# Retention attention in whole units, with smaller decay tables, and matmul operands at multiples of 512 bytes

## The chip, the cores and the metric

One NeuronCore of one Trainium2 chip. Times are microseconds (us) of device time for one execution. A measurement is the median of several runs.

## The reference, cut to what matters

Inputs: q, k and v with 4 batches, 8 heads, 576 positions and 64 dims, and the weights of two expert stages. All is float32.

```python
scores = matmul(q, k^T) / sqrt(64)
Dmat   = where(rel >= 0, gamma[h] ** rel, 0)      # rel = row - column, gamma[h] = 1 - 2**(-5-h)
x      = matmul(scores * Dmat, v)                 # no softmax; heads side by side: [2304, 512]
x      = relu(x @ w_in)**2 @ w_out                # first MoE: 512 -> 2048 -> 512
p      = probs / (sum(probs) + 1e-9)
out    = sum over 4 experts e of p[:, e] * (relu(x @ w1[e]) @ w2[e])     # 512 -> 1024 -> 512
```

## The kernel before

**Attention** (lines 136 to 334) takes two heads of a batch as a unit: 16 units, n = 0 to 15. Positions are cut in five chunks c of 128, the last of 64 (`CH`). As the decay is a power of gamma, the part of a chunk that looks at earlier chunks goes through a running state of 64x64 per head: `update` (L231) adds k^T v of a chunk to a state in PSUM with start and stop flags over four chunks, and two ScalarE copies (L248) take a snapshot of it, one for each head, before the next update adds to the same place. `outer` (L269) multiplies the snapshot with the scaled queries. The part inside a chunk is `scores` (L203), the decay mask by VectorE (`masked`, L218), and `inner` (L253), masked scores times v. `finish` (L281) rounds the sum to float32r on ScalarE (`xh`) and keeps the rest by a VectorE subtraction (`xl`). Heads j = 0 and 1 lie in the two halves of the partitions or of the columns.

A unit is done in two steps, h = 0 with chunks 0 to 2 and h = 1 with chunks 3 and 4. The loop from L309 issues for each step an update, the next step's scores and masks, the values of all chunks of the step but the last, a second update, the last chunk's values, the outer products, and `finish`. The fifth chunk's values use 64 of the 128 rows (L266). Scores have K = 64 rows, all other matmuls of attention 128.

`load` (L160) fetches a unit three ahead, from SyncE's queue (from ScalarE's for unit 0), into tiles with three buffers. In the first four units it also fetches that head pair's tables: a mask of 192 columns, whose last 64 repeat the first, and the query decay for 448 positions. `prepare` (L186) scales k and q on GpSimd. The expert weights arrive as float64 words: from unit 3 on `tick` advances a generator (L68, L101) that rebuilds them on VectorE, ScalarE and GpSimd, three steps per unit.

**MoE** (L356 on). Every operand is split into a high and a low float32r part, and each product is three matmuls. Weights go in 24 chunks c of two 128-wide slices of the inner dimension: 8 of the first MoE, 16 of the second. Tokens go in five groups g, four of 512 and one of 256. `layer1` (L365) has the weights w1 stationary and x moving, 24 matmuls a group. `layer2_1` (L389) has w2 stationary and the activations g moving, 24 matmuls. `layer2_2` (L418) has g stationary and w2 moving with 512 columns, six matmuls for each 128 tokens. Layer 2 of one group follows layer 1 of the next.

**Where tiles lie.** Pools are laid out one behind the other in each partition: 16 KB that are kept back, four constants of 32 bytes, then `xh` and `xl` (L42), the pieces of weights (`wrp`, `cvp`, `wp`), and then the tiles of attention, and in the same place, once it is over, those of MoE (L341 to L347): the accumulators, `pr` (288 bytes), `prsum` (96), and `ghi`, `glo`, `r`. In the built program xh starts at byte 16512, which is 32 x 512 + 128; the first buffer of whi at 123008, which is 240 x 512 + 128; the first of ghi at 193024, which is 377 x 512.

Of the kernel before, what the change touches and what calls it, by code (L numbers as in the profile page):

```python
# [6 lines left out]
F32 = mybir.dt.float32  # L7
# [3 lines left out]
ACTF = mybir.ActivationFunctionType  # L11
ALU = mybir.AluOpType
PSUM = bass.MemoryType.PSUM
# [19 lines left out]
def tile_kernel(ctx, tc, qT, kT, kn, vn, v4d, mask, qdec, kdec, wd, w, probs, out):  # L33
    nc = tc.nc
    const = ctx.enter_context(tc.tile_pool(name="const", bufs=1))
    xp = ctx.enter_context(tc.tile_pool(name="xp", bufs=1))
    wrp = ctx.enter_context(tc.tile_pool(name="wrp", bufs=4))
    cvp = ctx.enter_context(tc.tile_pool(name="cvp", bufs=1))
# [8 lines left out]
    def f32(ap):  # L47
        return ap.bitcast(F32)
# [87 lines left out]
    def attention(a):  # L136
# [3 lines left out]

        ap = a.enter_context(tc.tile_pool(name="ap", bufs=3))
        ac = a.enter_context(tc.tile_pool(name="ac", bufs=1))
        pq = a.enter_context(tc.tile_pool(name="pq", bufs=2, space=PSUM))
        px = a.enter_context(tc.tile_pool(name="px", bufs=2, space=PSUM))
        pst = a.enter_context(tc.tile_pool(name="pst", bufs=2, space=PSUM))

        mk = ac.tile([C, NP, 2, MW], F32, name="mk")
        qd = ac.tile([128, NP, S - C], F32, name="qd")
        kd = ac.tile([C, NP, 4, 2], F32, name="kd")
        v4 = ac.tile([64, B * NP, 2, D], F32, name="v4")  # L150

        kts = [ac.tile([128, NC_ * C], F32, name=f"kt{i}") for i in range(3)]

        sbs = [ac.tile([128, 2, D], F32, name=f"st{i}") for i in range(6)]

        units = [(b, a) for b in range(B) for a in range(NP)]
        NU = len(units)
# [2 lines left out]
        def load(n):  # L160
            if n >= NU:
                return
            b, a = units[n]
            q_t = ap.tile([128, S], F32, name="q_t")
            k_t = kts[n % 3]
            k_n = ap.tile([C, 4, 2, D], F32, name="k_n")
            v_n = ap.tile([C, 4, 2, D], F32, name="v_n")

            dma = nc.scalar if n == 0 else nc.sync
            nc.sync.dma_start(out=q_t, in_=qT[b, a])  # L170
            dma.dma_start(out=k_t[:, :S], in_=kT[b, a])
            if n == 0:
                dma.dma_start(out=kd, in_=kdec)
            if n < NP:
                nc.sync.dma_start(out=mk[:, a], in_=mask[:, a])
            dma.dma_start(out=k_n, in_=kn[b, a].rearrange("p (c h d) -> p c h d", c=4, h=2))
            nc.sync.dma_start(out=v_n, in_=vn[b, a].rearrange("p (c h d) -> p c h d", c=4, h=2))
            if a == 0:
                dma.dma_start(out=v4[:, b * NP : (b + 1) * NP], in_=v4d[b].rearrange("p (a h d) -> p a h d", a=NP, h=2))
            if n < NP:  # L180
                nc.sync.dma_start(out=qd[:, a], in_=qdec[:, a])
            tl[n] = (q_t, k_t, k_n, v_n)

        qs = {}

        def prepare(n):  # L186

# [7 lines left out]
            qs[n] = ap.tile([128, S - C], F32, name="q_s")  # L195
            nc.gpsimd.tensor_tensor(out=qs[n], in0=q_t[:, C:], in1=qd[:, a, :], op=ALU.mult)

        steps = [(n, h) for n in range(NU) for h in range(2)]
        CS = [(0, 1, 2), (3, 4)]
        qks, pts, sts, snaps = {}, {}, {}, {}  # L200
        snap_n = [0]

        def scores(s):  # L203
            n, h = s
            q_t, k_t, _, _ = tl[n]
            qk = pq.tile([C, 2, 512], F32, name="qk")
            for c in CS[h]:
                o, m = CH[c]
                w = o - CH[CS[h][0]][0]
                for j in range(2):  # L210
                    p = slice(64 * j, 64 * j + 64)
                    nc.tensor.matmul(  # L212
                        qk[:, j, w : w + m], k_t[p, o : o + C], q_t[p, o : o + m], start=True, stop=True,
                        skip_group_check=True,
                    )
            qks[s] = qk

        def masked(s):  # L218
            n, h = s
            a = units[n][1]  # L220
            qk = qks.pop(s)
            pt = ap.tile([C, 2, 3 * C], F32, name="pt")
            if h == 0:
                v = lambda t: t[:, :, : 3 * C].rearrange("p j (c i) -> p j c i", c=3)
                m = mk[:, a, :, :C].unsqueeze(2).to_broadcast([C, 2, 3, C])
                nc.vector.tensor_tensor(out=v(pt), in0=v(qk), in1=m, op=ALU.mult)
            else:
                nc.vector.tensor_tensor(out=pt[:, :, :MW], in0=qk[:, :, :MW], in1=mk[:, a], op=ALU.mult)  # L228
            pts[s] = pt

        def update(n, c):  # L231

            if n >= NU:
                return
            _, _, k_n, v_n = tl[n]
            if c == 0:
                sts[n] = pst.tile([128, D], F32, name="state")
            st = sts[n]
            for j in range(2):
                nc.tensor.matmul(  # L240
                    st[64 * j : 64 * j + 64, :], k_n[:, c, j, :], v_n[:, c, j, :],
                    start=(c == 0), stop=(c == 3), skip_group_check=True,
                )
            sb = sbs[snap_n[0] % len(sbs)]
            snap_n[0] += 1
            for j in range(2):
                p = slice(64 * j, 64 * j + 64)
                nc.scalar.copy(out=sb[p, j, :], in_=st[p, :])  # L248
            snaps[n, c + 1] = sb

        xos = {}

        def inner(s, c):  # L253

            n, h = s
            v_n = tl[n][3]
            o, m = CH[c]
            w = o - CH[CS[h][0]][0]
            if c == CS[h][0]:
                xos[s] = px.tile([128, 512], F32, name="xo")  # L260
            xo, pt = xos[s], pts[s]
            for j in range(2):
                vc = v_n[:, c, j, :] if c < 4 else v4[:, n, j, :]
                nc.tensor.matmul(  # L264
                    xo[64 * j : 64 * j + 64, w : w + m], vc, pt[:m, j, w : w + m],
                    start=(w == 0), stop=(c == 0), skip_group_check=True,  # L266
                )

        def outer(s, c):  # L269

            n, h = s
            o, m = CH[c]
            w = o - CH[CS[h][0]][0]
            xo, sb = xos[s], snaps.pop((n, c))
            for j in range(2):
                nc.tensor.matmul(  # L276
                    xo[64 * j : 64 * j + 64, w : w + m], sb[:, j, :], qs[n][:, o - C : o - C + m],
                    start=False, stop=True, skip_group_check=True,
                )

        def finish(s):  # L281
            n, h = s
            b, a = units[n]
            o = CH[CS[h][0]][0]
            m = sum(CH[c][1] for c in CS[h])
            xo = xos.pop(s)
            t = b * S + o
            hi = xh_[:, a, t : t + m]
            nc.scalar.copy(out=hi, in_=xo[:, :m])  # L289
            nc.vector.tensor_tensor(out=xl_[:, a, t : t + m], in0=xo[:, :m], in1=f32(hi), op=ALU.subtract)  # L290
            pts.pop(s)

        load(0)
        warm = ac.tile([1, 1], F32, name="warm")
# [1 line left out]
        nc.scalar.copy(out=warm, in_=warm)  # L296
        for t in kts:
            nc.vector.memset(t[:, S:], 0.0)
        for t in sbs:
            nc.gpsimd.memset(t, 0.0)  # L300
        load(1)
        load(2)
        prepare(0)
        scores(steps[0])
        masked(steps[0])
        update(0, 0)
        prepare(1)
        update(0, 1)
        for i, s in enumerate(steps):  # L309
            n, h = s  # L310
            nxt = steps[i + 1] if i + 1 < len(steps) else None
            un, uc = (n, 2) if h == 0 else (n + 1, 0)
            update(un, uc)
            if nxt:
                scores(nxt)
                masked(nxt)
            cs = CS[h]
            for c in cs[:-1]:
                inner(s, c)
            update(un, uc + 1)  # L320
            inner(s, cs[-1])
            for c in cs:
                if c:
                    outer(s, c)
            finish(s)
            if h == 0:
                prepare(n + 2)
            else:
                load(n + 3)
            if h == 0 and n % 2 == 0 and 2 <= n < 2 + 2 * PC:  # L330
                load_piece(0, n // 2 - 1)
            if s == (3, 0):
                work.append(split_w(0))
            tick(1 + h)

    with tc.manual_schedule():
        with ExitStack() as a:
# [7 lines left out]
        yacc = [yp.tile([128, KT, GS[g]], F32, name=f"y{g}", tag=f"acc{g}") for g in range(NG)]  # L345
        pr = yp.tile([128, NTT, 4], F32, name="pr")
        psum_ = yp.tile([128, NTT], F32, name="prsum")  # L347
        nc.sync.dma_start(out=pr, in_=probs)
        nc.vector.tensor_reduce(out=psum_, in_=pr, axis=mybir.AxisListType.X, op=ALU.add)
        nc.vector.tensor_scalar_add(psum_, psum_, 1e-9)  # L350
# [95 lines left out]
def _host(inputs):  # L446
# [28 lines left out]
    gamma = (1.0 - 2.0 ** (-5.0 - np.arange(H))).reshape(NP, 2)  # L475
    rel = np.arange(C)[None, :] - np.arange(C)[:, None]
    mask = np.where(rel[:, None, None, :] >= 0, gamma[None, :, :, None] ** np.abs(rel)[:, None, None, :], 0.0) / 8.0
    mask = np.concatenate([mask, mask[..., : MW - C]], axis=3)
    qdec = np.repeat(gamma, D, axis=1).T[:, :, None] ** (np.arange(C, S) - S // 2)[None, None, :] / 8.0
    pos = np.arange(4)[None, :] * C + np.arange(C)[:, None]  # L480
    kdec = gamma[None, :, None, :] ** (S // 2 - pos)[:, None, :, None]
    f = np.float32
# [25 lines left out]
```

## Time and profile before

| | |
|---|---|
| median of 3 runs | 1288.08 us (1287.55 to 1289.81) |
| profiled execution | 1288.76 us, span 1286.5 us |
| granted TensorE clock, mean | 0.999 |
| TensorE busy | 1272.8 us, 99% |
| VectorE, ScalarE, GpSimd busy | 658.7, 299.0, 332.9 us |
| chain of waits by engine | PE 97%, DVE 1%, DMA 1% |

In the profile PE is TensorE, PEld its weight loads, DVE VectorE, ACT ScalarE, POOL GpSimd, and SP SyncE's DMA queue. L365 is line 365 of the kernel. "h<-xh,whi" reads as the tile written, then the tiles read. A float32 matmul of attention appears as two passes per matmul, so an instruction group "x4" at L240 is one update for two heads. Matmuls overlap, and the duration of a single one is longer than the time from its start to the next one's.

### The profile page before, as it was taken

The numbers are of one execution on the slowest core, as the hardware profiler recorded it, in microseconds if no ns is written. First come the engines' busy times: TensorE is split into PE (matmuls) and PEld (weight loads), VectorE is DVE, ScalarE is ACT, GpSimd is POOL, SyncE is SP. The second block draws the span as 40 slices with busy tenths as digits, with TensorE's granted clock in tenths as the row PEclk, the third lists the DMA queues.
The fourth block names the chain that finished last, engine by engine and source line by source line (L and its number), as shares of the span: only waits on it lengthen the run. The fifth ranks groups of instructions, "written<-read, shape, count | busy, mean of one in ns | idle before, by whom it ended". The sixth has DMA issues, their size and how long they took to land.

```text
span 1286.5 us, 16159 instructions
## 1 busy us (share of the span) xinstructions
PE 1272.8 (99%) x6720; PEld 1059.2 (82%) x6720; DVE 658.7 (51%) x946; ACT 299.0 (23%) x636; POOL 332.9 (26%) x270
## 2 busy tenths in 40 slices
PE   7999999999999999999999999999999999999998
PEld 6878888888888888888888888888888888888887
DVE  4965777887877851143343433434434433434334
ACT  3544322223222253311111111111111111111110
POOL 4654454444444592011010010110110110110100
PEclk9999999999999999999999999999999999999999
DMA  9931110111110000000000000000000000000003
GB/s 330 327 105 34 38 61 23 44 50 33 49 47 28 25 33 25 9 33 24 10 33 11 22 33 9 25 29 12 25 25 9 34 25 9 33 17 17 1 34 114
DMA packets 27465, 59.42 MB, mean 46 GB/s; under 512 B 3328, under 2 KB 4352, under 8 KB 27392
## 3 DMA queue, kind: packets, MB, share of 16 engines
q1 hardware_dynamic: 26880, 57.69, 13.1%
q8 instruction: 52, 0.85, 0.3%
q10 hardware_dynamic: 512, 0.70, 0.2%
q14 instruction: 21, 0.17, 0.0%
HBM read 53.66 MB, written 4.72 MB: 45 GB/s over the span
## 4 chain that ended last, share of the span: by engine, by line
PE 97%; DVE 1%; DMA 1%; ACT 0%; issue 0%; ACTq 0%; DVEq 0%
PE h L365 46%; PE o L418 31%; PE o L389 16%; PE xo L264 1%; PE qk L212 1%; PE xo L276 1%; PE state L240 1%; DMA v_n<-vn 1%; DMA k_n<-kn 0%; DVE cv_e L82 0%; DVE cv_p L86 0%; DVE xl L290 0%; ACT xh L289 0%; DVE pt L228 0%; DVE cv_m L88 0%; DVE cv_e L84 0%
## 5 line engine op out<-in xcount | busy, mean ns | idle before, releaser
L365 PE MATMUL h<-xh,whi 128*128 128x512 f32 (+1 forms) x960 | 353.7, 368 | 0.8 <-DVE xl L290 0.8
L365 PE MATMUL h<-xh,wlo 128*128 128x512 f32 (+1 forms) x960 | 354.2, 369 | 0.0
L365 PE MATMUL h<-xl,whi 128*128 128x512 f32 (+1 forms) x960 | 353.3, 368 | 0.0
L375 DVE SCALAR_TENSOR_TENSOR glo<-h,ghi 128x512 fp32r<-128x512 f32 (+1 forms) x160 | 102.2, 638 | 354.7 <-ACT ghi L374 354.7
L426 DVE SCALAR_TENSOR_TENSOR oacc<-o,pr,oacc 128x512 f32<-128x512 f32 x270 | 202.6, 750 | 139.4 <-PE o L418 135.1
L122 POOL TENSOR_TENSOR wlo<-wraw,whi 128x512 fp32r<-128x512 f32 x64 | 82.7, 1293 | 645.7 <-ACT whi L121 616.5
L374 ACT ACTIVATE ghi<-h 128x512 fp32r<-128x512 f32 (+1 forms) x160 | 89.0, 556 | 644.0 <-PE h L365 644.0
L418 PE MATMUL o<-whi,ghi 128*128 128x512 f32 x576 | 227.8, 395 | 0.0
L418 PE MATMUL o<-wlo,ghi 128*128 128x512 f32 x576 | 227.4, 395 | 0.0
L418 PE MATMUL o<-whi,glo 128*128 128x512 f32 x576 | 227.3, 395 | 0.0
L365 PEld LDWEIGHTS h<-xh,whi 128*128 128x128 f32 x960 | 180.8, 188 | 32.7 <-DVE xl L290 1.0
L365 PEld LDWEIGHTS h<-xl,whi 128*128 128x128 f32 x960 | 180.7, 188 | 32.2
L365 PEld LDWEIGHTS h<-xh,wlo 128*128 128x128 f32 x960 | 180.7, 188 | 30.9
L372 POOL TENSOR_TENSOR glo<-r,ghi 128x512 fp32r<-128x512 f32 (+1 forms) x80 | 95.8, 1199 | 142.6 <-ACT ghi L371 142.6
L370 DVE TENSOR_TENSOR r<-r 128x512 f32<-128x512 f32 (+1 forms) x80 | 81.4, 1017 | 94.9 <-ACT r L369 94.9
L418 PEld LDWEIGHTS o<-wlo,ghi 128*128 128x128 f32 x576 | 108.5, 188 | 25.7
L418 PEld LDWEIGHTS o<-whi,glo 128*128 128x128 f32 x576 | 108.7, 189 | 24.6
L418 PEld LDWEIGHTS o<-whi,ghi 128*128 128x128 f32 x576 | 108.5, 188 | 24.3
L389 PE MATMUL o<-ghi,wlo 128*128 128x512 f32 (+1 forms) x320 | 119.4, 373 | 0.0
L389 PE MATMUL o<-glo,whi 128*128 128x512 f32 (+1 forms) x320 | 119.1, 372 | 0.0
L389 PE MATMUL o<-ghi,whi 128*128 128x512 f32 (+1 forms) x320 | 119.0, 372 | 0.0
L397 DVE TENSOR_TENSOR y<-o,y 128x512 f32<-128x512 f32 (+1 forms) x140 | 85.5, 627 | 8.1 <-PE o L389 7.4
(51 smaller groups left out, 937.6 us busy)
## 6 DMA issues: line engine op xcount, KB each, us to landing
wraw<-wd SPq DMA_DIRECT2D x32, 512.0 KB, 3.6
wraw<-w SPq DMA_DIRECT2D x64, 256.0 KB, 2.7
q_t<-qT SPq DMA_DIRECT2D x16, 288.0 KB, 5.2
out<-oacc SPq DMA_DIRECT2D x18, 256.0 KB, 2.0
kt<-kT SPq DMA_DIRECT2D x15, 288.0 KB, 5.4
v_n<-vn SPq DMA_DIRECT2D x16, 256.0 KB, 4.8
k_n<-kn SPq DMA_DIRECT2D x15, 256.0 KB, 5.4
qd<-qdec SPq DMA_DIRECT2D x4, 224.0 KB, 5.0
```

The costliest lines, as they stand in the source:

```text
L122: nc.gpsimd.tensor_tensor(out=lo[:, s], in0=r, in1=f32(hi[:, s]), op=ALU.subtract)
L212: nc.tensor.matmul(qk[:, j, w : w + m], k_t[p, o : o + C], q_t[p, o : o + m], start=True, stop=True, skip_group_check=True,)
L240: nc.tensor.matmul(st[64 * j : 64 * j + 64, :], k_n[:, c, j, :], v_n[:, c, j, :], start=(c == 0), stop=(c == 3), skip_group_check=True,)
L365: nc.tensor.matmul(h, a[:, f, k, :], x[:, k, :], start=(n == 0), stop=(n == 3 * KT - 1))
L370: nc.vector.tensor_tensor(out=r, in0=r, in1=r, op=ALU.mult)
L372: nc.gpsimd.tensor_tensor(out=lo[:, f, :], in0=r, in1=f32(hi[:, f, :]), op=ALU.subtract)
L374: nc.scalar.activation(out=hi[:, f, :], in_=h, func=ACTF.Relu)
L375: nc.vector.scalar_tensor_tensor(out=lo[:, f, :], in0=h, scalar=0.0, in1=f32(hi[:, f, :]), op0=ALU.max, op1=ALU.subtract)
L389: nc.tensor.matmul(o, a[:, f, 128 * m : 128 * m + 128], x[:, f, :], start=(n == 0), stop=(n == 3 * FT - 1))
L397: nc.vector.tensor_tensor(out=y, in0=o, in1=y, op=ALU.add)
L418: nc.tensor.matmul(o, a[:, f, 128 * m : 128 * m + 128], x[:, f, :], start=(n == 0), stop=(n == 3 * FT - 1))
L426: nc.vector.scalar_tensor_tensor(out=acc, in0=o, scalar=pr[:, tt, e : e + 1], in1=acc, op0=ALU.mult, op1=ALU.add)
```

## The change

- Attention works by whole units. `scores(n + 1)` and `masked(n + 1)` come at the start of unit n's turn, for all five chunks in one block. The four updates of unit n + 1 stand between the values and outer products of unit n. The state is one PSUM tile with a half for even and one for odd units. PSUM pools change to one buffer for each half of the scores; there are 8 snapshot tiles instead of 6.
- The fifth chunk's values use 128 rows: `v4` gets 128 partitions, the lower ones filled with zeros, and the masked scores there are zero as well.
- Tables: 128 columns of the mask are loaded, and 128 columns of query decay with three factors. `tables` expands them on ScalarE, five operations for each of the first four units.
- All four updates of unit 0 come ahead of the loop. The three steps of weight conversion of a unit come together at its end.
- Two tiles that nothing reads: `pad0` of 1920 bytes ahead of xh, and `pad1` of 128 bytes ahead of ghi.

```diff
@@ -33,6 +33,8 @@
 def tile_kernel(ctx, tc, qT, kT, kn, vn, v4d, mask, qdec, kdec, wd, w, probs, out):
     nc = tc.nc
     const = ctx.enter_context(tc.tile_pool(name="const", bufs=1))
+
+    const.tile([128, 480], F32, name="pad0")
...
         ac = a.enter_context(tc.tile_pool(name="ac", bufs=1))
-        pq = a.enter_context(tc.tile_pool(name="pq", bufs=2, space=PSUM))
+        pq = a.enter_context(tc.tile_pool(name="pq", bufs=1, space=PSUM))
         px = a.enter_context(tc.tile_pool(name="px", bufs=2, space=PSUM))
-        pst = a.enter_context(tc.tile_pool(name="pst", bufs=2, space=PSUM))
+        pst = a.enter_context(tc.tile_pool(name="pst", bufs=1, space=PSUM))
 
         mk = ac.tile([C, NP, 2, MW], F32, name="mk")
         qd = ac.tile([128, NP, S - C], F32, name="qd")
+        qw = ac.tile([128, NP, C + 3], F32, name="qw")
         kd = ac.tile([C, NP, 4, 2], F32, name="kd")
-        v4 = ac.tile([64, B * NP, 2, D], F32, name="v4")
-
+
+        v4 = ac.tile([C, B * NP, 2, D], F32, name="v4")
         kts = [ac.tile([128, NC_ * C], F32, name=f"kt{i}") for i in range(3)]
 
-        sbs = [ac.tile([128, 2, D], F32, name=f"st{i}") for i in range(6)]
+        sbs = [ac.tile([128, 2, D], F32, name=f"st{i}") for i in range(8)]
+
+        st_ = pst.tile([128, 2, D], F32, name="state")
 
         units = [(b, a) for b in range(B) for a in range(NP)]
...
@@ -171,17 +176,32 @@
             dma.dma_start(out=k_t[:, :S], in_=kT[b, a])
             if n == 0:
                 dma.dma_start(out=kd, in_=kdec)
+            dma.dma_start(out=k_n, in_=kn[b, a].rearrange("p (c h d) -> p c h d", c=4, h=2))
             if n < NP:
-                nc.sync.dma_start(out=mk[:, a], in_=mask[:, a])
-            dma.dma_start(out=k_n, in_=kn[b, a].rearrange("p (c h d) -> p c h d", c=4, h=2))
+                nc.sync.dma_start(out=mk[:, a, :, :C], in_=mask[:, a])
             nc.sync.dma_start(out=v_n, in_=vn[b, a].rearrange("p (c h d) -> p c h d", c=4, h=2))
+            if n < NP:
+                nc.sync.dma_start(out=qw[:, a], in_=qdec[:, a])
             if a == 0:
-                dma.dma_start(out=v4[:, b * NP : (b + 1) * NP], in_=v4d[b].rearrange("p (a h d) -> p a h d", a=NP, h=2))
-            if n < NP:
-                nc.sync.dma_start(out=qd[:, a], in_=qdec[:, a])
+                dma.dma_start(
+                    out=v4[: S - 4 * C, b * NP : (b + 1) * NP], in_=v4d[b].rearrange("p (a h d) -> p a h d", a=NP, h=2)
+                )
             tl[n] = (q_t, k_t, k_n, v_n)
 
         qs = {}
+
+        def tables(n):
+
+            if n >= NP:
+                return
+            a = units[n][1]
+            nc.scalar.copy(out=mk[:, a, :, C:], in_=mk[:, a, :, : MW - C])
+            for c in range(4):
+                o, m = CH[c + 1]
+                nc.scalar.activation(
+                    out=qd[:, a, o - C : o - C + m], in_=qw[:, a, :m], func=ACTF.Copy,
+                    scale=1.0 if c == 0 else qw[:, a, C + c - 1 : C + c],
+                )
 
         def prepare(n):
...
-            n, h = s
+        PO = [CH[cs[0]][0] for cs in CS]
+        PM = [sum(CH[c][1] for c in cs) for cs in CS]
+        qks, pts, snaps = {}, {}, {}
+
+        def scores(n):
+            if n >= NU:
+                return
             q_t, k_t, _, _ = tl[n]
-            qk = pq.tile([C, 2, 512], F32, name="qk")
-            for c in CS[h]:
-                o, m = CH[c]
-                w = o - CH[CS[h][0]][0]
-                for j in range(2):
-                    p = slice(64 * j, 64 * j + 64)
-                    nc.tensor.matmul(
-                        qk[:, j, w : w + m], k_t[p, o : o + C], q_t[p, o : o + m], start=True, stop=True,
-                        skip_group_check=True,
-                    )
-            qks[s] = qk
...
         def update(n, c):
 
             if n >= NU:
                 return
             _, _, k_n, v_n = tl[n]
-            if c == 0:
-                sts[n] = pst.tile([128, D], F32, name="state")
-            st = sts[n]
+            st = st_[:, n % 2, :]
             for j in range(2):
                 nc.tensor.matmul(
                     st[64 * j : 64 * j + 64, :], k_n[:, c, j, :], v_n[:, c, j, :],
                     start=(c == 0), stop=(c == 3), skip_group_check=True,
                 )
-            sb = sbs[snap_n[0] % len(sbs)]
-            snap_n[0] += 1
+            sb = sbs[(4 * n + c) % len(sbs)]
             for j in range(2):
                 p = slice(64 * j, 64 * j + 64)
                 nc.scalar.copy(out=sb[p, j, :], in_=st[p, :])
...
-            if c == CS[h][0]:
-                xos[s] = px.tile([128, 512], F32, name="xo")
-            xo, pt = xos[s], pts[s]
+            w = o - PO[h]
+            if w == 0:
+                xos[n, h] = px.tile([128, 512], F32, name=f"xo{h}", bufs=2 - h)
+            xo, pt = xos[n, h], pts[n, h]
             for j in range(2):
                 vc = v_n[:, c, j, :] if c < 4 else v4[:, n, j, :]
                 nc.tensor.matmul(
-                    xo[64 * j : 64 * j + 64, w : w + m], vc, pt[:m, j, w : w + m],
+                    xo[64 * j : 64 * j + 64, w : w + m], vc, pt[:, j, w : w + m],
                     start=(w == 0), stop=(c == 0), skip_group_check=True,
...
         nc.scalar.copy(out=warm, in_=warm)
         for t in kts:
             nc.vector.memset(t[:, S:], 0.0)
+        nc.vector.memset(v4[S - 4 * C :], 0.0)
         for t in sbs:
             nc.gpsimd.memset(t, 0.0)
         load(1)
         load(2)
+        scores(0)
+        tables(0)
         prepare(0)
-        scores(steps[0])
-        masked(steps[0])
-        update(0, 0)
+        masked(0)
+        for c in range(4):
+            update(0, c)
+        tables(1)
         prepare(1)
-        update(0, 1)
-        for i, s in enumerate(steps):
-            n, h = s
-            nxt = steps[i + 1] if i + 1 < len(steps) else None
-            un, uc = (n, 2) if h == 0 else (n + 1, 0)
-            update(un, uc)
-            if nxt:
-                scores(nxt)
-                masked(nxt)
-            cs = CS[h]
-            for c in cs[:-1]:
-                inner(s, c)
-            update(un, uc + 1)
-            inner(s, cs[-1])
-            for c in cs:
-                if c:
-                    outer(s, c)
-            finish(s)
-            if h == 0:
-                prepare(n + 2)
-            else:
-                load(n + 3)
-            if h == 0 and n % 2 == 0 and 2 <= n < 2 + 2 * PC:
+        for n in range(NU):
+            scores(n + 1)
+            masked(n + 1)
+            inner(n, 0, 0)
+            inner(n, 0, 1)
+            update(n + 1, 0)
+            inner(n, 0, 2)
+            outer(n, 0, 1)
+            update(n + 1, 1)
+            outer(n, 0, 2)
+            finish(n, 0)
+            inner(n, 1, 3)
+            inner(n, 1, 4)
+            update(n + 1, 2)
+            outer(n, 1, 3)
+            update(n + 1, 3)
+            outer(n, 1, 4)
+            finish(n, 1)
+            tables(n + 2)
+            prepare(n + 2)
+            load(n + 3)
+            if n % 2 == 0 and 2 <= n < 2 + 2 * PC:
                 load_piece(0, n // 2 - 1)
-            if s == (3, 0):
+            if n == 3:
                 work.append(split_w(0))
-            tick(1 + h)
+            tick(3)
...
@@ -345,6 +367,7 @@
         yacc = [yp.tile([128, KT, GS[g]], F32, name=f"y{g}", tag=f"acc{g}") for g in range(NG)]
         pr = yp.tile([128, NTT, 4], F32, name="pr")
         psum_ = yp.tile([128, NTT], F32, name="prsum")
+        yp.tile([128, 32], F32, name="pad1")
         nc.sync.dma_start(out=pr, in_=probs)
...
     mask = np.where(rel[:, None, None, :] >= 0, gamma[None, :, :, None] ** np.abs(rel)[:, None, None, :], 0.0) / 8.0
-    mask = np.concatenate([mask, mask[..., : MW - C]], axis=3)
-    qdec = np.repeat(gamma, D, axis=1).T[:, :, None] ** (np.arange(C, S) - S // 2)[None, None, :] / 8.0
+
+    gq = np.repeat(gamma, D, axis=1).T[:, :, None]
+    qdec = np.concatenate(
+        [gq ** (np.arange(C, 2 * C) - S // 2)[None, None, :] / 8.0, gq ** (C * np.arange(1, 4))[None, None, :]], axis=2
+    )
```

In `scores`, `masked`, `inner`, `outer` and `finish` the rest is a change of indices.

## Rows read from the trace of the kernel before

**Rows 1.** The chain that ended last, by line (share of the span).

```profile
PE h L365 46%; PE o L418 31%; PE o L389 16%; PE xo L264 1%; PE qk L212 1%; PE xo L276 1%; PE state L240 1%; DMA v_n<-vn 1%; DMA k_n<-kn 0%; DVE cv_e L82 0%; DVE cv_p L86 0%; DVE xl L290 0%; ACT xh L289 0%; DVE pt L228 0%; DVE cv_m L88 0%; DVE cv_e L84 0%
```

**Rows 2.** The chain in order of time (start us, us, what): two scores blocks, attention's end.

```profile
40.73 0.87 PE qk L212 x12
...
78.88 0.87 PE qk L212 x12
...
83.59 0.53 PE xo L276 x8
...
84.91 0.50 PE h L365
```

**Rows 3.** The chain in the second MoE, 600 to 640 us.

```profile
601.27 5.46 PE h L365 x24
606.73 5.59 PE o L418 x24
...
623.36 2.86 PE h L365 x24
```

**Rows 4.** The chain in the first MoE, 96 to 152 us.

```profile
96.10 5.59 PE o L389 x24
...
137.72 2.88 PE o L389 x24
```

**Rows 5.** TensorE's timeline inside one block of L365 (start, duration, engine, line).

```profile
702.66 0.39 PE L365 MATMUL h<-xh,wlo 128*128 128x512 f32 x1
...
705.61 0.39 PE L365 MATMUL h<-xh,whi 128*128 128x512 f32 x1
```

**Rows 6.** The chain through one unit of attention, 28.9 to 33.3 us.

```profile
28.91 0.26 PE xo L264 x4
29.18 0.48 PE xo L276 x8
29.66 0.18 PE state L240 x4
...
30.43 0.59 PE xo L264 x8
...
31.14 0.22 PE xo L264 x4
...
31.91 0.87 PE qk L212 x12
32.78 0.37 PE xo L264 x4
33.15 0.11 PE state L240 x4
```

**Rows 7.** Busy us by window: length, PE, PEld, DVE, ACT, POOL, PEclk, DMA share, GB/s.

```profile
40.00:60.00 20.00, 18.88 (x310) 16.48 (x308) 18.71 (x28) 10.44 (x44) 15.09 (x12) 1.00 0.98 346
```

**Rows 8.** Groups by line and shape: count, busy us, mean ns, idle before.

```profile
L365 PE MATMUL h<-xh,wlo 128*128 128x512 f32 x768 | 300.0, 391 | 0.0
...
L418 PE MATMUL o<-whi,ghi 128*128 128x512 f32 x576 | 227.8, 395 | 0.0
```

**Rows 9.** Timeline of two updates and the copies between them.

```profile
79.95 0.28 PE L240 MATMUL state<-v_n,k_n 128*64 128x64 f32 x4
...
80.33 0.44 ACT L248 COPY st<-state 64x64 f32<-64x64 f32 x2 [0.71 <-PE state L240]
...
80.82 0.34 PE L240 MATMUL state<-v_n,k_n 128*64 128x64 f32 x4
```

**Rows 10.** The chain through the first updates.

```profile
7.44 0.51 PE state L240 x4
...
9.34 0.22 ACT st L248
...
9.60 0.48 PE state L240 x4
```

**Rows 11.** Timeline, GpSimd's first scaling of queries and what released it.

```profile
8.05 1.13 POOL L196 TENSOR_TENSOR q_s<-q_t,qd 128x448 f32<-128x448 f32 x1 [6.38 <-DMA qd<-qdec]
```

More of the change, by code (lines that the diff above doesn't have):

```diff
@@ L196, in prepare @@
             nc.gpsimd.tensor_tensor(out=qs[n], in0=q_t[:, C:], in1=qd[:, a, :], op=ALU.mult)
-        steps = [(n, h) for n in range(NU) for h in range(2)]
         CS = [(0, 1, 2), (3, 4)]
-        qks, pts, sts, snaps = {}, {}, {}, {}
-        snap_n = [0]
-        def scores(s):
-            n, h = s
-            q_t, k_t, _, _ = tl[n]
-            qk = pq.tile([C, 2, 512], F32, name="qk")
-            for c in CS[h]:
-                o, m = CH[c]
-                w = o - CH[CS[h][0]][0]
-                for j in range(2):
-                    p = slice(64 * j, 64 * j + 64)
-                    nc.tensor.matmul(
-                        qk[:, j, w : w + m], k_t[p, o : o + C], q_t[p, o : o + m], start=True, stop=True,
-                        skip_group_check=True,
-                    )
-            qks[s] = qk
@@ L218, in masked @@
-        def masked(s):
-            n, h = s
-            a = units[n][1]
-            qk = qks.pop(s)
-            pt = ap.tile([C, 2, 3 * C], F32, name="pt")
-            if h == 0:
-                v = lambda t: t[:, :, : 3 * C].rearrange("p j (c i) -> p j c i", c=3)
-                m = mk[:, a, :, :C].unsqueeze(2).to_broadcast([C, 2, 3, C])
-                nc.vector.tensor_tensor(out=v(pt), in0=v(qk), in1=m, op=ALU.mult)
-            else:
-                nc.vector.tensor_tensor(out=pt[:, :, :MW], in0=qk[:, :, :MW], in1=mk[:, a], op=ALU.mult)
-            pts[s] = pt
+        PO = [CH[cs[0]][0] for cs in CS]
@@ new lines, in attention @@
+        PM = [sum(CH[c][1] for c in cs) for cs in CS]
[3 more added lines that the diff above has]
+                return
+            q_t, k_t, _, _ = tl[n]
+            for h in range(2):
+                qk = pq.tile([C, 2, 512], F32, name=f"qk{h}")
+                for c in CS[h]:
+                    o, m = CH[c]
+                    w = o - PO[h]
+                    for j in range(2):
+                        p = slice(64 * j, 64 * j + 64)
+                        nc.tensor.matmul(
+                            qk[:, j, w : w + m], k_t[p, o : o + C], q_t[p, o : o + m], start=True, stop=True,
+                            skip_group_check=True,
+                        )
+                qks[n, h] = qk
@@ new lines, in masked @@
+        def masked(n):
+            if n >= NU:
+                return
+            a = units[n][1]
+            for h in range(2):
+                qk = qks.pop((n, h))
+                pt = ap.tile([C, 2, PM[h]], F32, name=f"pt{h}", bufs=2)
+                if h == 0:
+                    v = lambda t: t[:, :, : 3 * C].rearrange("p j (c i) -> p j c i", c=3)
+                    m = mk[:, a, :, :C].unsqueeze(2).to_broadcast([C, 2, 3, C])
+                    nc.vector.tensor_tensor(out=v(pt), in0=v(qk), in1=m, op=ALU.mult)
+                else:
+                    nc.vector.tensor_tensor(out=pt, in0=qk[:, :, :MW], in1=mk[:, a], op=ALU.mult)
+                pts[n, h] = pt
@@ L251, in attention, with inner @@
         xos = {}
-        def inner(s, c):
-            n, h = s
+        def inner(n, h, c):
             v_n = tl[n][3]
             o, m = CH[c]
-            w = o - CH[CS[h][0]][0]
-            if c == CS[h][0]:
-                xos[s] = px.tile([128, 512], F32, name="xo")
-            xo, pt = xos[s], pts[s]
+            w = o - PO[h]
+            if w == 0:
+                xos[n, h] = px.tile([128, 512], F32, name=f"xo{h}", bufs=2 - h)
+            xo, pt = xos[n, h], pts[n, h]
             for j in range(2):
@@ L264, in inner, with outer @@
                 nc.tensor.matmul(
-                    xo[64 * j : 64 * j + 64, w : w + m], vc, pt[:m, j, w : w + m],
+                    xo[64 * j : 64 * j + 64, w : w + m], vc, pt[:, j, w : w + m],
                     start=(w == 0), stop=(c == 0), skip_group_check=True,
                 )
-        def outer(s, c):
-            n, h = s
+        def outer(n, h, c):
             o, m = CH[c]
-            w = o - CH[CS[h][0]][0]
-            xo, sb = xos[s], snaps.pop((n, c))
+            w = o - PO[h]
+            xo, sb = xos[n, h], snaps.pop((n, c))
             for j in range(2):
@@ L279, in outer, with finish @@
                 )
-        def finish(s):
-            n, h = s
+        def finish(n, h):
             b, a = units[n]
[L284 to L291, printed above, removed]
+            xo = xos.pop((n, h))
+            t = b * S + PO[h]
+            hi = xh_[:, a, t : t + PM[h]]
+            nc.scalar.copy(out=hi, in_=xo[:, : PM[h]])
+            nc.vector.tensor_tensor(
+                out=xl_[:, a, t : t + PM[h]], in0=xo[:, : PM[h]], in1=f32(hi), op=ALU.subtract
+            )
+            pts.pop((n, h))
         load(0)
@@ L302, in attention @@
         load(2)
+        scores(0)
+        tables(0)
         prepare(0)
-        scores(steps[0])
-        masked(steps[0])
-        update(0, 0)
+        masked(0)
+        for c in range(4):
+            update(0, c)
+        tables(1)
         prepare(1)
-        update(0, 1)
-        for i, s in enumerate(steps):
-            n, h = s
-            nxt = steps[i + 1] if i + 1 < len(steps) else None
-            un, uc = (n, 2) if h == 0 else (n + 1, 0)
-            update(un, uc)
-            if nxt:
-                scores(nxt)
-                masked(nxt)
-            cs = CS[h]
-            for c in cs[:-1]:
-                inner(s, c)
-            update(un, uc + 1)
-            inner(s, cs[-1])
-            for c in cs:
-                if c:
-                    outer(s, c)
-            finish(s)
-            if h == 0:
-                prepare(n + 2)
-            else:
-                load(n + 3)
-            if h == 0 and n % 2 == 0 and 2 <= n < 2 + 2 * PC:
+        for n in range(NU):
[20 more added lines that the diff above has]
+            if n % 2 == 0 and 2 <= n < 2 + 2 * PC:
                 load_piece(0, n // 2 - 1)
-            if s == (3, 0):
+            if n == 3:
                 work.append(split_w(0))
-            tick(1 + h)
+            tick(3)
     with tc.manual_schedule():
@@ L477, in _host @@
     mask = np.where(rel[:, None, None, :] >= 0, gamma[None, :, :, None] ** np.abs(rel)[:, None, None, :], 0.0) / 8.0
-    mask = np.concatenate([mask, mask[..., : MW - C]], axis=3)
-    qdec = np.repeat(gamma, D, axis=1).T[:, :, None] ** (np.arange(C, S) - S // 2)[None, None, :] / 8.0
+    gq = np.repeat(gamma, D, axis=1).T[:, :, None]
+    qdec = np.concatenate(
+        [gq ** (np.arange(C, 2 * C) - S // 2)[None, None, :] / 8.0, gq ** (C * np.arange(1, 4))[None, None, :]], axis=2
+    )
     pos = np.arange(4)[None, :] * C + np.arange(C)[:, None]
```

## The prediction

> **What bounds the kernel now.** I read the chain of waits first: TensorE carries 97% of it, and nearly all of that lies on L365, L418 and L389, the matmuls of the two expert stages (called MoE below) [rows 1]. They start at 84.91 us [rows 2] and run to the end, so attention is 85 us of 1286.5 and MoE is 1200. In MoE the chain is a row of blocks without a gap. 24 matmuls of the first layer (L365) on 512 columns take 5.46 us, 24 of the second layer (L418) on as many columns 5.59 [rows 3]; L389, the second layer of the first MoE, also takes 5.59 [rows 4]. So the reader is to see two speeds for one shape: 227.5 and 232.9 ns a matmul. Inside a block of L365, 13 steps from 702.66 to 705.61 are 2.95 us, 226.9 ns each [rows 5]. With 256 columns the layers hardly differ: 2.86 and 2.88 [rows 3, 4].
>
> Attention is three things at once. A unit of it on TensorE takes 33.15 + 0.11 - 28.91 = 4.35 us [rows 6]; from unit 7 to unit 15 the scores at 40.73 and 78.88 are eight units apart, 4.77 each [rows 2], because VectorE is then busy 18.71 of 20 us and the DMA engines 98% [rows 7].
>
> **The operands of MoE.** The two pads shift every later tile by 1920 bytes, and what follows the second by 2048. In the built program of before, xh starts at byte 16512 of a partition and the pieces of w at 123008: both 128 past a multiple of 512. ghi starts at 193024, a multiple. All their slices step by multiples of 512 bytes. So L365 reads both operands at +128, L389 has w at +128 and g at 0, L418 has g at 0 and w at +128. Equal offsets go with 227.5 ns, unequal ones with 232.9, whichever operand is stationary. After the change all are at 0: equal everywhere. I take it that what counts is whether the stationary load of the next matmul and the moving stream of this one start alike within 512 bytes. Then:
> - second layer: 768 matmuls of L389 (8 chunks x 4 groups x 24) and 3 x 576 of L418 [rows 8] are 32 + 72 = 104 blocks of 24; each goes from 5.59 to 5.46: 104 x 0.13 = 13.5 us.
> - both layers: a block at 226.9 ns throughout is 5.445. If the slower steps at the head of each block come from the change of offset between layers, the 200 blocks of 512 columns (L365 has 3 x 768 / 24 = 96, [rows 8]) gain 0.02 each, 4 us. I take half.
> Sum: 15.5 us off. TensorE waits for nobody in MoE, so all of it counts. Bounds: 0 if offsets are not the cause, 17.5 if all steps reach 226.9; beyond both, see the rivals.
>
> [...]
>
> **Attention, TensorE's own work.** From [rows 6], a set of four passes costs 0.22 us at 128 columns (L264 at 31.14) and 0.11 at 64 (state, 33.15). What is above that is the switch between K=64 and K=128: scores x12 0.87 for 0.66, the first values after scores 0.59 for 0.44 and 0.37 for 0.22, the fifth chunk 0.26 for 0.11 and the outer set behind it 0.48 for 0.33, state before scores 0.18 for 0.11. Whole units do the scores in one block and give the fifth chunk all 128 rows. Passes: scores 0.99, values 0.99, outer 0.77, four updates 0.44, sum 3.19; one switch in and out 0.21 + 0.15 + 0.07 = 0.43. That is 3.62 instead of 4.35.
>
> **Attention, the updates.** Each update adds into the same PSUM tile that ScalarE must have copied first, both copies. Update at 79.95, copies from 80.33 for 0.44, next update at 80.82: a hop of 0.87 us [rows 9]. At the start, with nothing else to do, it is 1.08 (7.44 to 9.60 in two hops), and an update starts only after the second copy (9.34 + 0.22, then 9.60) [rows 10]. In the old order the four updates lie a half unit or so apart. In the new one, from one update to the next TensorE has: 0.11 + inner 0.22 + outer 0.22 = 0.55, so it stalls 0.32; then 0.11 + 0.22 + 0.22 + 0.11 = 0.66, stall 0.21; then 0.11 + 0.22 = 0.33, stall 0.54. TensorE is in order: behind a waiting update stand the outer products, then the next scores. ScalarE's cast in finish lies between the second and third pair of copies and fits in the hop. Period: 3.62 + 1.07 = 4.69, 0.34 more than before where TensorE set the pace, and just under the 4.77 where VectorE did. VectorE's work per unit is the same (two masks, two subtractions, three conversion steps), now with the three steps together; it had almost no idle time, so I put the later eight units at 4.77.
>
> **Attention, head and sum.** The decay tables shrink (mask 192 to 128 KB, qdec 224 to 66 KB per unit, by their shapes), 0.9 MB less, 2.6 us of DMA at the 346 GB/s of a stretch where it is full [rows 7]. Nothing in TensorE's chain waited for the loads of units 1 to 3, so I count this at nothing; its cover is TensorE's 4.35 a unit. The tables are expanded by five ScalarE operations per unit, ahead of the state copies in ScalarE's queue. In units 1 to 3 they fall into the time between the last cast and the next copies. In unit 0 they stand before the first copy and wait for the query table, which in the old kernel let GpSimd go at 8.05 [rows 11]; the first copy is due when the update of 7.44 is done, 0.51 later [rows 10]. Four operations, each above the 0.22 of a 64-column copy, are at least 0.9 us, of which a smaller table wins some back: 0.5 late. Updates at 7.44 and then 1.08 apart put the fourth at 10.68; with its 0.5 and the 0.5 late, scores of unit 1 start at 11.7 (the old kernel had only the first half of unit 0's scores done by then, this one all). Then 15 x 4.69 = 70.35, eight units at 0.08 more = 0.64, the last unit's values 1.9, and the 0.79 from the end of the last values (83.59 + 0.53) to the first L365 at 84.91 [rows 2]: 85.4. Before: 84.9. So +0.5 us. Below: if an update waits only for its own half's copy, the hop falls by 0.23 and the first seven units by about 0.6: -5. Above: if the masks queue behind the three conversion steps in 11 units and lose 0.35 each: +4.
>
> **Sum.** The profiled execution took 1288.76 us (span 1286.5 and 2.26 around it), 0.68 above the median. 1288.76 - 15.5 + 0.5 - 0.68 = 1273.1.
>
> **Rivals.**
> 1. *Offsets are not the cause.* The layers differ also in where their tiles lie: x fills 16 to 90 KB of a partition, w and g both lie above 120 KB. If streams disturb each other by region, all stays at 5.59. For it: the 256-column blocks are alike in both layers. Against: nothing in the rows. Then attention alone decides: 1288.08 + 0.5 = 1288.6, from 1283 to 1293.
> 2. *A start at a multiple of 512 is the cost (slower).* Every slow form has one operand at 0, and the only fast form has none. If it is this, L365 goes from 5.46 to 5.59 when x and w move to 0: 96 x 0.13 = 12.5 us, second layer unchanged: 1301. It decides as soon as L365's steady step leaves 226.9 upward. Against: an operand that starts at a boundary crosses fewer of them.
> [...]
>
> [...]
>
> **Chances.** Forecast 0.55, its own range 1266 to 1279 (13.5 to 17.5 off, attention -5 to +4). Rival 1 0.22, rival 2 0.12, rival 3 0.11. The range 1266 to 1292 leaves out rival 2, most of rival 3 and rival 1's end. A measurement of this kernel can tell about 0.2% (2.6 us) from no change. Faster: 0.55 + 0.11 and a few hundredths of rival 1, 0.68. Same: most of rival 1, 0.14. Slower: rival 2 and the bad end of rival 1, 0.18.
>
> **What would show it.** Forecast: L389 and L418 blocks at 5.45, L365 at 5.45 without slower steps at its head; MoE from first L365 to the end 15 us shorter. Attention: TensorE idle before state, released by ScalarE's copies, some 1.1 us a unit; scores in one block of 20 passes; first L365 near 85.4. [...] A unit of 4.0 would show that the hop was read wrongly.

## The result and the profile after

Median 1277.01 us (4 runs, 1276.35 to 1279.18) against 1288.64 in the same runs for the kernel before: ratio 0.9913, 95% interval 0.9895 to 0.993. The forecast was 1273.1. The profiled execution took 1279.18 (span 1277.2), 9.6 less than that of before.

The two parts moved in opposite directions. MoE, from its first matmul to the end of the span, went from 1286.5 - 84.91 = 1201.6 us to 1277.2 - 92.45 = 1184.75: 16.85 off. Attention ends 7.54 later. The chain of waits in MoE, as in [rows 3] (start, us, what; L388 is now layer 1, L441 layer 2):

```profile
601.91 5.44 PE h L388 x24
607.35 5.44 PE o L441 x24
...
623.67 2.87 PE h L388 x24
```

and in the first MoE, as in [rows 4] (L412 is its layer 2):

```profile
103.63 5.44 PE o L412 x24
...
144.61 2.87 PE o L412 x24
```

All blocks of 512 columns are alike, 5.44 us, and 5.47 right behind a block of 256 columns; those of 256 columns nearly kept their time (2.87, before 2.86 and 2.88). A quiet unit of attention (one that waits for nothing but the state copies), which was 4.35 us in [rows 6], is 4.86: scores start at 28.02, 32.88 and 37.74. The timeline of TensorE and ScalarE in it:

```profile
34.63 0.28 PE L263 MATMUL state<-v_n,k_n 128*64 128x64 f32 x4
...
35.02 0.44 ACT L270 COPY st<-state 64x64 f32<-64x64 f32 x2 [1.30 <-PE state L263]
...
35.51 0.34 PE L263 MATMUL state<-v_n,k_n 128*64 128x64 f32 x4 [0.15 <-ACT st L270]
...
35.94 0.44 ACT L270 COPY st<-state 64x64 f32<-64x64 f32 x2 [0.49 <-PE state L263]
...
36.41 0.48 ACT L306 CAST xh<-xo 128x384 fp32r<-128x384 f32 x1
36.43 0.34 PE L263 MATMUL state<-v_n,k_n 128*64 128x64 f32 x4
...
36.87 0.44 ACT L270 COPY st<-state 64x64 f32<-64x64 f32 x2
...
37.36 0.34 PE L263 MATMUL state<-v_n,k_n 128*64 128x64 f32 x4 [0.37 <-ACT st L270]
```

The reader is to see the four updates (L263) 0.88, 0.92 and 0.93 us apart, the last three each right behind a pair of copies. What TensorE waited for (first 92 us: total, times, longest):

```profile
PE state L263 <- ACT st L270: 10.4, 31, 1.1
```

In [rows 9] the hop was 0.87. An update that had to wait takes 0.34 instead of 0.28, its copies start 0.43 after it instead of 0.38, and so each further hop is 0.05 longer.

The longest turns of the loop are 5.84 and 6.40 us, from 47.71. The chain there is VectorE's conversion steps, then the mask that queued behind them, then the scores that waited for its buffer:

```profile
48.94 1.24 DVE cv_e L82
50.20 1.16 DVE cv_e L84
51.39 1.24 DVE cv_e L86
52.63 0.88 DVE pt L251
53.55 2.30 PE qk L235 x20
```

The 20 passes took 2.30 us instead of 1.26, and TensorE's granted clock over them is 0.53. The window before, in which TensorE was idle a quarter of the time, and the one after (length, PE, PEld, DVE, ACT, POOL, PEclk, DMA share, GB/s):

```profile
47.70:53.50 5.80, 4.38 (x76) 3.54 (x72) 4.85 (x6) 3.17 (x13) 4.64 (x5) 1.00 1.03 375
53.90:57.30 3.40, 3.40 (x38) 3.28 (x38) 3.37 (x6) 0.08 (x1) 2.37 (x2) 0.53 0.72 260
```

The other three executions have a mean granted clock of 0.999 to 1.000 (this one 0.998) and are 2.0 to 2.8 us shorter, so part of the 7.54 belongs to this execution alone.

### The profile page after: what moved, and what is told of

Same layout as the page of the kernel before. It is cut to its first block, busy times and chain, and to the rows that moved or that the text cites. A ratio compares the mean times of both kernels' runs of the same rounds, so it can differ in the third digit from the quotient of the medians.

```text
span 1277.2 us, 16187 instructions
## 1 busy us (share of the span) xinstructions
PE 1255.4 (98%) x6720; PEld 1054.5 (83%) x6720; DVE 650.7 (51%) x947; ACT 306.5 (24%) x656; POOL 332.8 (26%) x272
## 4 chain that ended last, share of the span: by engine, by line
PE 95%; ACT 3%; DVE 1%; issue 1%; DMA 0%; SPq 0%; ACTq 0%
PE h L388 46%; PE o L441 31%; PE o L412 15%; ACT st L270 2%; PE qk L235 1%; PE state L263 1%; ACT xh L306 1%; PE xo L285 1%; DMA qw<-qdec 0%; ACT qd L201 0%; DVE xl L307 0%; PE xo L296 0%; DVE cv_e L86 0%; DVE cv_e L82 0%; DVE cv_m L92 0%
## 5 line engine op out<-in xcount | busy, mean ns | idle before, releaser
L388 PE MATMUL h<-xh,whi 128*128 128x512 f32 (+1 forms) x960 | 353.2, 368 | 0.8 <-DVE xl L307 0.8
L388 PE MATMUL h<-xl,whi 128*128 128x512 f32 (+1 forms) x960 | 353.2, 368 | 0.0
L388 PE MATMUL h<-xh,wlo 128*128 128x512 f32 (+1 forms) x960 | 353.1, 368 | 0.0
L441 PE MATMUL o<-whi,ghi 128*128 128x512 f32 x576 | 224.3, 389 | 0.0
L441 PE MATMUL o<-whi,glo 128*128 128x512 f32 x576 | 224.3, 389 | 0.0
L441 PE MATMUL o<-wlo,ghi 128*128 128x512 f32 x576 | 224.1, 389 | 0.0
L388 PEld LDWEIGHTS h<-xh,whi 128*128 128x128 f32 x960 | 181.0, 189 | 31.6 <-DVE xl L307 1.0
L388 PEld LDWEIGHTS h<-xl,whi 128*128 128x128 f32 x960 | 180.9, 188 | 30.5
L388 PEld LDWEIGHTS h<-xh,wlo 128*128 128x128 f32 x960 | 180.9, 188 | 30.0
L393 DVE TENSOR_TENSOR r<-r 128x512 f32<-128x512 f32 (+1 forms) x80 | 78.3, 979 | 95.9 <-ACT r L392 95.9
L441 PEld LDWEIGHTS o<-wlo,ghi 128*128 128x128 f32 x576 | 108.1, 188 | 22.5
L441 PEld LDWEIGHTS o<-whi,ghi 128*128 128x128 f32 x576 | 108.2, 188 | 22.1
L441 PEld LDWEIGHTS o<-whi,glo 128*128 128x128 f32 x576 | 108.2, 188 | 21.9
L412 PE MATMUL o<-glo,whi 128*128 128x512 f32 (+1 forms) x320 | 117.8, 368 | 0.0
L412 PE MATMUL o<-ghi,whi 128*128 128x512 f32 (+1 forms) x320 | 117.8, 368 | 0.0
L412 PE MATMUL o<-ghi,wlo 128*128 128x512 f32 (+1 forms) x320 | 117.7, 368 | 0.0
L420 DVE TENSOR_TENSOR y<-o,y 128x512 f32<-128x512 f32 (+1 forms) x140 | 85.9, 628 | 11.2 <-PE o L412 9.8
```

What stands on the lines that cost most here:

```text
L388: nc.tensor.matmul(h, a[:, f, k, :], x[:, k, :], start=(n == 0), stop=(n == 3 * KT - 1))
L393: nc.vector.tensor_tensor(out=r, in0=r, in1=r, op=ALU.mult)
L412: nc.tensor.matmul(o, a[:, f, 128 * m : 128 * m + 128], x[:, f, :], start=(n == 0), stop=(n == 3 * FT - 1))
L420: nc.vector.tensor_tensor(out=y, in0=o, in1=y, op=ALU.add)
L441: nc.tensor.matmul(o, a[:, f, 128 * m : 128 * m + 128], x[:, f, :], start=(n == 0), stop=(n == 3 * FT - 1))
```

## The experiments: operands

**Each half of the change alone.** The old kernel with the two pads, and the changed one without them.

```diff
 # pads_only: the old kernel
+    const.tile([128, 480], F32, name="pad0")
+        yp.tile([128, 32], F32, name="pad1")
 # no_pads: the changed kernel
-    const.tile([128, 480], F32, name="pad0")
-        yp.tile([128, 32], F32, name="pad1")
```

> The old attention with the two pads alone. Theory: the pads are worth all that MoE gained between the two profiles (1201.6 - 1184.75 = 16.9 us) and the new attention costs the rest. Then every MoE block of 512 columns is at 5.44 us, attention still ends near 84.9, and the time is 1288.6 - 16.9 = 1271.7. Rival: part of MoE's gain came from the new attention (the weights converted at another time); then blocks stay partly at 5.59 and the time is above 1274.

> The changed kernel without its two pads. Theory: MoE returns to 5.46 (layer 1) and 5.59 (layer 2), attention ends near 90 to 92, and the time is 1277.0 + 16.9 = 1293.9, slower than before by 5 us. Rival (the new attention costs nothing, the pads gain only 11.6): 1288.6.

Measured: pads alone 1271.91 us, ratio 0.9865 (0.9848 to 0.9881); attention alone 1293.98, ratio 1.0037 (1.0024 to 1.005). With the pads alone both layers are at 5.44 (L420 layer 2, L367 layer 1); with the attention alone they are at 5.59 and 5.46 (L438, L385):

```profile
599.93 5.44 PE o L420 x24
605.37 5.44 PE h L367 x24
```

```profile
602.41 5.59 PE o L438 x24
608.00 5.46 PE h L385 x24
```

MoE starts at 85.04 and 91.66. Both theories held to 0.3 us: the pads are worth 17, the new attention costs 5.

**Is it the difference of the offsets?** The old kernel with other pads: one in front of the weights (`padc`, in the pool `cvp`) and one in front of the activations. The numbers are words of 4 bytes, `padc` first.

```diff
 # swap_offsets: 96 and 32;  all_at_128: none and 32
 # offsets_256_64: 64 and 48;  offsets_32_192: 8 and 80
+    cvp.tile([128, 96], F32, name="padc")
+        yp.tile([128, 32], F32, name="pad1")
```

> Old kernel with x at +128 and w and g at 0 (96 words of padding in front of the weights, 32 in front of the activations). Theory of equal offsets: the layers change places. Layer 1 now has unequal offsets and takes 5.59 a block, layer 2 equal ones and takes 5.44; time near 1288.6 + 96 x 0.13 - 104 x 0.15 = 1285.5. Rival (regions, or something else of the layers): layer 1 stays at 5.46. Rival (an operand at 0 is good in itself): layer 1, with one at 0 instead of none, gets no slower.

> Old kernel with x, w and g all 128 bytes past a multiple of 512 (one pad of 32 words in front of the activations). Theory of equal offsets: the same 5.44 in both layers as with all at 0, time near 1271.7. Rival (multiples of 512 matter): layer 2 stays at 5.59 or above, as none of its operands is at a multiple now, and layer 1 at 5.46.

Measured 1286.91 and 1272.62, one run each, as for the next two; the reading rests on the blocks. In the first the layers changed places (chain; L367 layer 1, L420 layer 2):

```profile
600.14 5.59 PE h L367 x24
605.73 5.45 PE o L420 x24
```

With all at 128, no operand at a multiple of 512, both layers are at 5.44 (L366, L419):

```profile
600.52 5.44 PE o L419 x24
605.96 5.44 PE h L366 x24
```

So neither the layer, nor its region, nor a multiple of 512 as such sets the speed, but the difference. The next two ask which differences:

> Old kernel with x at 128, w at 384, g at 448 within 512 bytes: layer 1's operands 256 apart, layer 2's 64 apart. If any difference within 512 bytes costs the same as 128 did, all blocks of 512 columns take 5.59. If what counts is where the two streams meet, the two distances give different times, and 64 lies nearer to 5.44.

> Old kernel with x at 128, w at 160, g at 352 within 512 bytes: layer 1's operands 32 apart, layer 2's 192 apart. Any difference costs the same: all blocks 5.59. Distance matters: layer 1 at or near 5.44, layer 2 at 5.59 or above.

Measured 1286.84 and 1294.56. The chains of the first and of the second (L391 is layer 2 of the first MoE):

```profile
106.83 5.51 PE o L391 x24
...
609.58 5.47 PE h L367 x24
615.04 5.60 PE o L420 x24
```

```profile
108.74 5.60 PE o L391 x24
...
600.88 5.50 PE o L420 x24
606.37 5.59 PE h L367 x24
```

Neither expectation fits as written: 256 apart is as good as equal, and the same distance gives two times according to which operand is stationary. Taken as stationary start minus moving start, modulo 256, all the blocks seen fall into line:

| difference mod 256 | block, us | where |
|---|---|---|
| 0 | 5.44 to 5.49 | layer 1 before and at 256 (up to 5.49 behind a layer with another difference); layer 2 swapped; all at 0; all at 128 |
| 32 | 5.59 to 5.60 | layer 1 at 32 |
| 64 | 5.59 to 5.60 | L420 at 64, L391 at -192 |
| 128 | 5.58 to 5.59 | L389 and L418 before; layer 1 swapped |
| 192 | 5.49 to 5.51 | L420 at 192, L391 at -64 |

The differences 0 and 256, 64 and -192, and 192 and -64 were each seen in both forms; 32 was seen in one place alone.

## The experiments: attention

All are edits of the changed kernel, pads included, but for the last.

**A shorter hop.** The second head's snapshot copy is left out.

```diff
-            for j in range(2):
+            for j in range(1):
                 nc.scalar.copy(out=sb[p, j, :], in_=st[p, :])
```

> The changed kernel without the second of the two state copies, so the second head's snapshots stay zero; nothing else is left out. Theory of the hop: from one update to the next it falls by 0.23 us to about 0.69, and the three stalls of a unit from 1.24 to about 0.45; undisturbed units take 4.05 to 4.2 instead of 4.86. Rival (a unit's length comes from the order of passes or from VectorE): 4.86 stays.

Measured: quiet units 4.17 us, 1269.67 us (one run). Updates at 31.95, 32.59, 33.31 and 33.98, hops of 0.64, 0.72 and 0.67:

```profile
31.95 0.28 PE L263 MATMUL state<-v_n,k_n 128*64 128x64 f32 x4
...
32.59 0.34 PE L263 MATMUL state<-v_n,k_n 128*64 128x64 f32 x4
...
33.98 0.34 PE L263 MATMUL state<-v_n,k_n 128*64 128x64 f32 x4
```

MoE starts at 82.80. The copies set the length of a quiet unit.

**Updates further apart.** `spread` puts the first update ahead of the scores; `carry` leaves the last for the next turn.

```diff
 # spread, in the loop (the four old places go)
+            update(n + 1, 0)
             scores(n + 1)
             masked(n + 1)
+            update(n + 1, 1)
             inner(n, 0, 0)   # to inner(n, 0, 2)
+            update(n + 1, 2)
             outer(n, 0, 1)   # outer(n, 0, 2), finish(n, 0)
+            tables(n + 2)
+            prepare(n + 2)
             inner(n, 1, 3)   # inner(n, 1, 4)
+            update(n + 1, 3)
             outer(n, 1, 3)   # outer(n, 1, 4), finish(n, 1)
 # carry: the same, with these in the four places; tables and prepare stay at the end;
 # ahead of the loop three updates of unit 0 instead of four
+            update(n, 3)
+            update(n + 1, 0)
+            update(n + 1, 1)
+            update(n + 1, 2)
```

> The changed kernel with the four updates of the next unit moved apart: the first ahead of the scores, the second behind them, the third behind the values of chunks 0 to 2, the fourth behind those of chunks 3 and 4; tables and prepare go behind the first finish, as the first update now comes earlier. Theory (TensorE stalls for the state copies, 1.24 us of each 4.86 us unit): the stalls go, a unit takes about 3.8 us where VectorE has no conversion steps and 4.5 to 4.8 where it has; MoE starts at 82 to 84 instead of 92 (90 without the clock's drop), time 1268 to 1271. Rival (VectorE's masks and conversion set the pace of the units): units stay near 4.86, time 1277.

> The changed kernel with the updates in other places: the fourth of a unit at the start of that unit's own turn, ahead of the scores; the first behind the scores, the second behind the values of chunks 0 to 2, the third behind those of chunks 3 and 4; prepare stays at the end of a unit, so GpSimd has the scores' 1.35 us for it. Theory of the hop: the waits that are left are about 0.05, 0.05 and nothing, a quiet unit takes 3.7 to 3.9 us, the long units behind VectorE 4.5 to 5; MoE starts at 81 to 84, time 1268 to 1271. Rival (GpSimd's scaling or VectorE hold each unit, as when the updates were spread): 4.35 and above, 1275 to 1277.

Both expectations missed. `spread`: 1277.29, ratio 0.9906 (0.9891 to 0.9921), like the change itself. The rival's time came, but not its reason: quiet units are 4.35. Before the first update TensorE now waits, 0.30 us in quiet turns. In long turns the wait is for GpSimd's scaling of k. At 48.40 that stood behind GpSimd's own conversion work (chain):

```profile
46.07 0.50 POOL wlo L101
...
47.30 1.05 POOL k_n L214
...
48.40 0.34 PE state L263 x4
```

In the longest turn, 5.97 us from 62.20, GpSimd itself had waited 3.83 us for the load of k, and TensorE then waited 1.92 for GpSimd (timeline). The DMA share from 62 to 68 us is 1.02:

```profile
66.81 1.04 POOL L214 TENSOR_TENSOR k_n<-k_n,kd 128x512 f32<-128x512 f32 x1 [3.83 <-DMA k_n<-kn]
...
67.90 0.34 PE L263 MATMUL state<-v_n,k_n 128*64 128x64 f32 x4 [1.92 <-POOL k_n L214]
```

`carry`: 1273.45, ratio 0.9878 (0.9862 to 0.9895), 3.6 us under the change. Its quiet units are 4.31 where I expected 3.7 to 3.9; I had left out that the update carried over still waits for the copies of the third, with the cast between them:

```profile
29.22 0.30 PE state L263 x4
...
30.05 0.42 ACT xh L306
...
30.52 0.21 ACT st L270
30.75 0.22 ACT st L270
30.96 0.04 issue
31.01 0.34 PE state L263 x4
```

**Conversion steps and tables.**

```diff
 # tick_split; the append at n == 3 moves up, behind masked(n + 1)
             finish(n, 0)
+            tick(1)
...
-            tick(3)
+            tick(2)
 # full_tables
-                nc.sync.dma_start(out=qw[:, a], in_=qdec[:, a])
+                nc.sync.dma_start(out=qd[:, a], in_=qdec[:, a])   # mask and host likewise
-        tables(...)
```

> The changed kernel with one of the three conversion steps of a unit behind the first finish instead of all three at its end. Theory: the three steps together, up to 3.7 us, delay the masks behind them and cost the long units 8 and 9 (5.84 and 6.40 in the trace) and the clock's drop behind them; split, those fall under 5.2, 1 to 2.5 us less, 1275. Rival (VectorE is simply full there): the same delay appears elsewhere, 1277.

> The changed kernel with the whole tables loaded as before the change, and no expansion on ScalarE. Theory: the expansion costs only in unit 0, where the first state copy waits behind it (8.72 instead of 8.0), and the 0.9 MB of loads saved were hidden anyway: 0.5 to 0.8 us faster, 1276.3. Rival (the loads saved are on the path): the units 1 to 4 wait for DMA and the time rises by up to 2.6 us, 1279.6.

`tick_split`: 1277.99 (0.9913, 0.9899 to 0.9928). Units 8 and 9 came down to 4.85, and one of 6.33 appeared further on (from 72.28). So the delay came up elsewhere, as the rival said, but not from a full VectorE: this turn waited 1.25 us for GpSimd, which is busy 5.92 of the 6 us from 72 to 78, VectorE 4.04. The chain there:

```profile
72.94 1.27 POOL wlo L101
74.22 1.19 POOL k_n L214
...
75.45 0.36 PE state L263 x4
```

`full_tables`: 1277.21 (0.9908, 0.9892 to 0.9925). The first copy came at 8.25 instead of 8.72, but the whole can't be told from the change: loads and expansion both cost nothing that shows, and the rival's 1279.6 is not seen.

**The part that pays, on the old attention.**

```diff
 # the old kernel with both pads
+        v4 = ac.tile([C, B * NP, 2, D], F32, name="v4")    # lower rows zero
-  vc, pt[:m, j, w : w + m],
+  vc, pt[:, j, w : w + m],
```

> The old attention with the two pads, and of the new attention only the fifth chunk's values on all 128 rows (v4 with 128 partitions, zeros below). Theory: the switch between K=64 and K=128 around that chunk costs 0.15 + 0.15 us a unit; where TensorE sets the pace (some seven units) that goes, where VectorE does it doesn't: MoE starts near 83 instead of 85.0, time 1271.9 - 2 = 1269.9. Rival (an update's wait for the state copies, which now comes closer behind the last one, takes the place): 1271.9.

Measured 1270.53, ratio 0.9861 (0.9847 to 0.9876); MoE starts at 82.97. The sign is as expected, but against 1271.91 for the pads alone it is less than the runs can tell. Both beat the change, by 5.1 and 6.5 us. The rival shows in part: where the fifth chunk went by faster (at the end of attention the outer products behind it took 0.46 us, with the pads alone 0.53), the update behind it now waits for ScalarE:

```profile
20.46 0.22 ACT st L249
20.68 0.04 issue
20.72 0.34 PE state L241 x4
```

## Why the prediction was right, and where not

- *Operands, -15.5.* Measured -16.85, between the taken value and its bound of 17.5: the slow steps at the head of a block did go, of which I had taken half. The theory, equal offsets, held in four arrangements (before, all at 0, swapped, all at 128). Too narrow was "within 512 bytes": 256 apart layer 1 took 5.45 to 5.49, so it is 256, and an equal start is one case of it. Unequal starts also don't all cost the same: 5.49 to 5.51 at 192, 5.58 to 5.60 at 32, 64 and 128. Rival 1 is refuted by the swap (layer 1 at 5.59, layer 2 at 5.45 to 5.48). Rival 2 is refuted by 5.44 in both layers with all at 0; all at 128 would have been fast by it too. Rival 3, a time far below the forecast's, had 0.11 by an estimate that no run shows: no block of 512 columns that was read in any run took less than 5.44.
- *TensorE's own work and the stalls.* That the updates would stall for the copies was right, the unit of 4.69 was not: 4.86. The failed step is the hop of 0.87, read from a pair whose first update had not waited: three hops are 2.73 us instead of 2.61. The other 0.05 is the block of scores, 1.26 for the 0.99 + 0.21 in the sum. Ten quiet turns at 0.17 are 1.7 us.
- *Head.* Scores of unit 1 at 11.7 were forecast and came at 11.75. The first turn was then counted as a steady one; it took 6.55 (11.75 to 18.30), 1.9 us more. TensorE still went at about half its later pace at the start of it (20 passes in 2.33 us, later 1.26). [rows 10] had a sign of it, 0.48 to 0.51 us an update where [rows 9] has 0.28 to 0.34. The granted clock of 11.75 to 14.08 is 1.00 in the profile, so why it was slow stays open.
- *Later units.* I kept VectorE's old 4.77 for eight units. They took 41.72 / 8 = 5.2 (42.61 to 84.33) with the clock's fall. The three long turns (5.10, 5.84, 6.40) and the turn of 5.01 from 84.33 are 3.6 above 4.69 each, and the end behind it took 3.11 where I had 1.9 + 0.79. That is 4.0, of which I had allowed 0.64. The terms, 1.9 + 1.7 + 3.4, make up the 7.05 between 85.4 and 92.45, all of the profiled execution.
- The sum of attention, +0.5 with an upper bound of +4, was thus mis-sized: +5 by the medians (1277.01 - 1271.91), outside that bound; by the interval of the attention alone (0.24% to 0.50%) it is 3.1 to 6.4. The time stayed in the range because of MoE, in part by luck. The lower bound of -5 was loose as well: seven units at 0.6 are 4.2.

How the starts of the two operands come to set the time was not seen in the traces; only the times by difference are shown.

## What to carry to other kernels

Where one shape of matmul runs at two speeds in one trace, compare the start of its stationary and its moving operand early: one pad of 128 bytes (`all_at_128`) gave the whole gain here (1272.62 us, with both pads 1271.91). When moving a producer-consumer hop into a shorter stretch, count what the engine has to do between two of them and read the hop where it already binds (here 0.92 and 0.93 us, not 0.87). And test the parts of a change apart: half of this one was a loss that the other half hid.

## What was not expected of the hardware

In these runs the time of 24 float32r matmuls with 128x128 weights and 512 columns went with the difference of the operands' starts modulo 256 bytes, by up to 2.9% (5.44 to 5.60), and with a sign: at 192 it is 0.06 above that at 0, at 64 0.16. Blocks of 256 columns hardly notice: 2.84 to 2.88. And a stretch of 5.8 us with a quarter of it idle was followed by 3.4 us at a granted clock of 0.53. Of the two turns there, the first was 0.98 us longer than a quiet one, by the wait for VectorE's mask, and the second 1.54, at the lower clock.
